# Linear attention followed by an MoE layer on one core: v of the first two batches moved to SyncE's queue, matmuls on zeros ahead of the first transposes, and a new order

## The chip, the cores and the metric

The kernel runs on one core of a Trainium2 chip. The metric is the device time of one execution in microseconds (us). A core has five engines that run beside each other and wait for each other by semaphores: TensorE (PE; its weight loads are listed apart as PEld), VectorE (DVE), ScalarE (ACT), GpSimd (POOL) and SyncE (SP). [...]

## The reference

```python
def phi(x):                                   # per head, w_phi is 64 x 128
    proj = einsum('bhsd,df->bhsf', x, w_phi)
    proj = proj - max(abs(proj), axis=-1, keepdims=True)
    return concatenate([exp(proj), exp(-proj)], axis=-1)
q_p, k_p = phi(q), phi(k)                     # q, k, v: 8 batches x 8 heads x 576 x 64, fp32
kv  = einsum('bhsf,bhsd->bhfd', k_p, v)
z   = sum(k_p, axis=2)
num = einsum('bhsf,bhfd->bhsd', q_p, kv)
den = einsum('bhsf,bhf->bhs', q_p, z)[..., None] + 1e-06
x   = (num / den) as 4608 tokens x 512        # heads side by side
h   = x @ w_in                                # 512 x 2048
g   = where(h > 0, h, exp(min(h, 0)) - 1)
out = g @ w_out                               # 2048 x 512
```

## The kernel before

**Tiling.** A *quad* is four heads of one batch; there are 16, two for each batch, quads 2b and 2b+1. A head's 576 rows are 512 main rows and a tail of 64. A *chunk* is 512 tokens: the main rows of batch b are chunk b, all the tails together are chunk 8. All matmuls take bf16.

**One quad.** k and q (`k_b`, `q_b`, cast to bf16 by POOL's DMAs) are transposed to `kT`, `qT`: in quads 0 to 4 by PE (tile `tr`, tail `trt`, L530 and L534) with a copy out of PSUM by DVE or ACT (L538, L542), from quad 5 on by SP's transposing DMAs (L504, L510). PE projects k (`pk`, L558), DVE takes the largest absolute value (`m_k`, L585), ACT the exponentials `EK`, `EKt` (L604). From `m_k` ACT makes the factors `em` (L649); POOL copies them (L663) and scales v with them into `vs` (L672, six operations for each quad, four large and two small). q is projected twice, with the rows on the partitions for the maximum `m_q` (L558 and L576) and with the features on them (`pq`, L702 and L714) for the exponentials `Eq`, `Eqt` (L753). Then PE makes `pkv` (L785), ACT or DVE copies it to `kv` (L799), PE makes `pn` and `pnt` (L833, L848), DVE weighs and adds the parts into `tot` (L868, L874), divides (`den`, `rec`, L906, L907), and DVE or POOL writes x (L911). x is transposed to `xT` by PE in batches 0 and 1 (L963, L967, copies L971, L975), by SP later.

**One chunk.** Sixteen times: four matmuls `ph` of w_in with `xT` (L1014), the exponential `e_sb` on ACT (L1026), minus one on POOL (`u_sb`, L1030), the ELU into `gT` on DVE (L1037). Then `po`, 64 matmuls of `gT` with w_out (L1080), copies to `o_sb` and stores by SP (L1112, L1116). A chunk's `ph` need both quads of its batch.

**The order.** Nothing is scheduled at run time. A class `Planner` holds a list of operations, each with a cost for each engine that may run it, what it depends on, and a rank from a table written out in the code (`RANKS`, 2140 two-digit numbers). While the program is built it goes through a modelled time: whenever an engine is free it takes the operation of lowest rank whose inputs the model says are there. So the ranks and the model's constants (`COLD`, `COLD_TIMES`, `LANDING`, ...) fix each engine's queue. On the chip each engine works through its queue in order; an instruction that waits holds up all behind it on its engine.

**Loads.** `load` (L427) puts loads on POOL's queue, each behind the one before: first k, q and v of batch 0 in halves of four heads (parts 0 and 2) with the tails (part 1, two DMAs) between, then k of batch 1, four parts of w_in, q of batch 1, four parts of w_in, w_out. `load_v` (L433) puts v of batches 1 to 7 on SP's queue. `hold(b)` (L1204), for b from 1, lets DVE write a column of the v tile from a maximum of quad 2b-1 (L1211), so that SP's load of v of batch b waits until then. v stays fp32 in SBUF.

**Start.** Before the planned part SP loads w_phi twice, and DVE clears w_phi_both, casts w_phi into it (L1148) and clears `EKts`, `Eqts` and a column of `tot` (L1145 to L1151).

Of the kernel before, what the change touches and what calls it, by code (L numbers as in the profile page):

```python
# [8 lines left out]
FP32 = mybir.dt.float32  # L9
# [22 lines left out]

DIGITS = "0123456789ABCDEFGHIJKLMNOPQRSTUVWXYZabcdefghijklmnopqrstuvwxyz+-"
RANKS = (
    "5L1J7b5G3Z4s4qD27p1C557m4k4m1E565q1G5tA-1TBCBQ1L4c51Bt1Q4x193m0P136l1X1K4F2o9g7X"
    "7k0r3G0O2y7l7n1W80Nh4K32Eg0L3972711D4e3Q5l1V3N5v3S5r14345n4w5z4a1U15Js2lHP6U3xCM"
    "0T2-1P1O7N1q6j6N0M4J2u0H3O2r0z29CG3A4bBS0n5kAE0k2788B31l091Y1r1k1dAl2O4I7EAj211j"
    "6R9x6q1h3p70MoAD8H1B8c5O9wHN7wAO9zJ5HY2bMuB6BD2vAwBGBkA+BMB116Mt8+CI2Y6n2w17829W"
    "316VBHEj2x916iC62K2C0Q4L8x33Bv222t4H0i5T4U0F5o6bHK1S7G5R5CDA4ZBl1w5X0c2S2j5W4C5Y"
    "8t1F9r2+1a1n3gBn3T636vIL3Y101b570w7PAUA20U7SCf3t0Z745D6w0l264g003K6KAH2n3k7KAN4G"  # L40
    "8a2kFn0-3j7o9a4dGM5-AT7J1t5sFa7I0A504vJE3J3h4M4-E7JZ8CDkCq5Z0E5ICb6d9o0B0G59FE8O"
    "3V4r2L2E2Z5A28371I5H443U7q1H0J3r2M2g2I2d353H9Z3q6z0u4Q423F3C3d8f3c3W1y0o3-3w3sHk"
    "68Ax462e2Q6t3B3a3I476hBy1-K930Ak20B-3z4A6k1A6J240+6B9-4B1+Ck050C2N0f7F5+0h1p4uNv"
# [12 lines left out]
    "DyDlJLMCJmD4EGCeCx2aMyQSE1JUHEBL5c7s9q6rEIAeMIAJ1mMKC56+3eECBVIiGyMRBNO1ARAXIYCu"
    "L2Es9iLWMzDWOYO2Tx927YK09SALTb9pVCEOLvTa84NC9B4nEtCnIUEeC1MkGkHjDpDsVMAqHwF3I5Do"
    "WcThC7GLGFD6AbMqFzF4L-FJEAFbITBjQP3lB49tO-FW4+ImFxA1LTEJA6IoGiEFF2HXGcHg437QBg6S"
    "G9L9E+Dh2mCaNnLk4RJ0NVFq0a8pApHb1cVXNdE08gKVNXCm6TL0OfHQGUHIDaFr9GCdOdHqDOKWNFHl"
    "GlKiF8LK1oL4AFGBKoJ8QfKhC-I1OTJYNLKP9LO7OuPSOHSzEdVZMnRuNyL1UkNjQBM9OMRtJhT2RxS8"  # L60
    "P5GeK6GfM16Z6fLrM7D9EaCgLHIbRK7-HSFAPa0y6CH3787vU9J4FQWZ12GHRQ9R2G8JJ1HzEmP4OjRh"
    "KDFu3DKBEK5h2s9kO+AhLlELJv0S3XBFD5HpIIQ61xKMJFINJ9HHJ-I+Cr3+JpBXPmJVA5JNH4A3IWFt"
    "CtMZIKE4Gx6LDYHGJSCoNzIGHTFIInHJMvWYLbEc9d9JWiJRCBJkUvEZRFWI73FfJuEUB5Q9IuI6E-90"
    "KLEXEMSMJcM4CCBEC9ENLoNBBIIFB2QyL7NAGoRlOyIfHiCSJqJXC3KILp9+KrLiBPJoM3NKLcMUA9OP"
    "SBHuVmQ8PYHU8FMmOqEP8b5QETLzGZPfNcO9DG7aPBKN1ZWsQeNr2TH8OnKg0DI3NIHZ7uIZNZNu1zJa"
    "4oNYOXLDOSISIrMYP3KFSaKRNmLf0mBoGuQ3GK7R5bRM5gIjGtKY8THvBBM+LGLmMaL3UbW2V-JdORQW"
    "LVRpVgLQUdUDLNOwPxTmP0UsUrEBKJHA53KHKGChPu6aKnIpL+SVWCMpQ5DrIsE6TuTrWaMwX1X2LnLg"
    "9YROX6MJWxIcCHCyGmR9KlHoK7M8N3TyWyK3FXEpTnN1Tt75I4D0D+H+MEWhI0H-QrK4H2P6JDMTP23n"
    "MdNoSYMF5pLXNfPOHFN59vIOFYGYO3QONR6xIAKtFKEVVTV8BOJgWUVASNP1QzUOUEJx8sVfRINNMHTg"
    "UHOJX7GqKUJMRgI2IhJQQ1I7N0WjWqIkExIlRbN276Lx7iIBIJUJPAJwEyG0QtIaI-MAL8MS4fIVMQGJ"  # L70
    "OUJjAf7DMxA4LZMG8NMORXG5V5JCHCQFDZD-PvLwCwHxNMFRDI6EO6LOOF9sNqPPDLIvDXJb0bItFdLq"
    "Fj9nOLHROELEQaLh2zVsOiNe8nKbOpRCGaBfPwPpGNPcNQQ2FeXGP8N+FsPbClLeDj8QNgLaTIIyNpNW"
    "H5UnPgPTKpVIVuO8R+S+TwT9UYSGVvTUJWP+U3WTUjSiTKFVHnOsEQTBOkK-86LAKsH0SoX8QwM5WnPi"
    "M2RZW5M-XBIRW3WmX0NaVPWOSdTdNJHdMPG1MVGpHfGCTRTkMeMrRBHyVcDbDmMgWQVJO5MbQEDdOrVQ"
    "MBPzN-QKJORnHWPXRy3LSs9mOxSu5wUGPjRE4ES1UuT3JtRiUzQkUcIPPkMcFFI8WETfTlS2SHWoSqPt"
    "WlWdV3PGWGRJUINETzQGVNUtWpRfPFDER7RNV7FGG4RrMhTiRHE2V9FSQbMfWMU1VaF5H1DwRDX5VSV6"
    "SFRcLFRmR5S78wKEMiA8KdSC4tSPShSELRSjOoWzLyU4KAMMSARd8SWeG-RGBpJ3MDKCEbWvOcOIGWKS"
    "O4QRFiVl8WPKD1XPOvQVFOPlP9O07CLLCUSOGzLJQhUM8eXIPDRUCRVrEoSr8oVWFgQ+2VXHQcKaF+Kc"
    "NbN4GTXFXQOb2WIwPHPLVeOGVdTpVFVxUaR0TsPyU0PeSXPMRYWBJePoUVN7VtUBWHRLG7GnMNH9MWKw"
    "KyStUqGbVkUlWXQUWwWkVnNxWfXKW8URXOW+WKRkWWXRXMUAVEVjGgMlCPFkW0K2IHQMSyTPWFQAULGd"  # L80
    "FPSxSIWAW6ERI9RoPsVBG2W-NGUpV+UZVoNkSJTLSmB8RTSTTHSeOOW1T7RWDCT0HaUCVVQjSpKjICSD"
    "L5U8SKWbU+U7NHSbSUS3VRQHVpPhScRRN9QiTcUyM0NOV1CjDfR1RaIeQuAaEwCsT4X3SZPqWuSlWPT5"
    "RPU5QNL6QvTOSnU6TVHVNiToVOQpLMHrWDU-S5X9TASgWgXCS0TJTXQoSSUoSkW7VHQsUxQmDqWJNTPZ"
    "GGR2H6PJFLUXR4RwCcIdGvQIUmIzPCMsTDQYQCPnDUQqQlQ-IXXANUT1FhXEOZUSDgTYF-QnQ7WtQ0VL"
    "8qTFW9RAGXIqFMV4R-WNOQWLVyWrPdPVEvX4VwVDM6OVTMSvTZTEONN6UTTvQTS-SQR3P7UKUQTeUeUw"
    "VzSwVUUU8iVbTCQQGjXLVKSRD8WVOtTNUiQxMjSWF1ViNtPUCYXJOhRS8YUNQdPIF0VqNsS4C+HtRvP-"
    "FmKZOaUWT6KvGrRe06XDNwTGS9KzQgLPFcXNQJOW8VUgQZUhR8T-OeTTVGVYRzT8TqWRTSSLVhT+UfW4"
    "UFV0U2UPTjRqOzRVTWV2TQRsK10g255EAtQXJzLj"
)


# [34 lines left out]
class Planner:  # L126
# [1 line left out]
    OWN = {"PE": 0.17, "ACT": 0.12, "DVE": 0.1, "POOL": 0.04, "SP": 0.0}  # L128
    LAG = {"PE": 0.25, "ACT": 0.2, "DVE": 0.13, "POOL": 0.07, "SP": 0.0}

    COLD = 46.0
    COLD_TIMES = 1.4

    CHANGE = 0.095

    MB_PER_US = 0.37
    MB_PER_US_OF_ONE = 0.26
    LANDING = 3.2

    AHEAD = 8  # L140

# [26 lines left out]
    def run(self):  # L168
# [9 lines left out]
        dma = 0.0  # L178
# [54 lines left out]
        while todo:  # L233
            started = False
            for e in ready:
# [37 lines left out]
                o.seen = o.end + self.LAG[e]  # L273
                if o.load:
                    took = o.load / self.MB_PER_US
                    o.seen = max(o.end + o.alone, dma + took + self.LANDING)
                    dma = max(dma, o.end) + took
                    if e == "POOL":
                        landed += [o.seen] * (2 if c > 1.2 else 1)
                for bank in o.uses:  # L280
# [29 lines left out]
def kernel(  # L310
# [111 lines left out]


    landed = {}
    swdge = [None]

    def load(name, mb, cost, fn, deps=()):  # L427

        o = add({"POOL": cost}, fn, deps, behind=[swdge[0]], key=-6.0, load=mb)
        swdge[0] = o  # L430
        landed[name] = o

    def load_v(name, mb, cost, fn, deps):  # L433
        landed[name] = add({"SP": cost}, fn, deps, key=-2.0, load=mb)
# [10 lines left out]
    def plan_loads(b):  # L445

        plan.slot = 2.0 * b - 2
        for n in range(2):
            deps = [o for g in range(2) for o in quads[2 * b - 4 + g]["tr"][n]]
            load(  # L450
                (b, n, 0),
                1.05,
                0.9,
                lambda e, n=n: load_main(nc.gpsimd, n, b, 0, 8),
                deps,
            )
            load((b, n, 1), 0.13, 1.26, lambda e, n=n: load_tails(nc.gpsimd, n, b))
            landed[b, n, 2] = landed[b, n, 0]
        deps = [o for g in range(2) for o in quads[2 * b - 4 + g]["vs"]]
        load_v((b, 2, 0), 1.05, 0.45, lambda e: load_main(nc.sync, 2, b, 0, 8), deps)  # L460
        load_v((b, 2, 1), 0.13, 0.8, lambda e: load_tails(nc.sync, 2, b), deps)
        landed[b, 2, 2] = landed[b, 2, 0]

    def plan_quad(i):
# [90 lines left out]
        def project(n, hh, bank):  # L555
            pk = psum(bank, [P, 4, F], FP32, "pk")
            for j in range(2 if hh < 4 else 1):
# [4 lines left out]
                    start=True,  # L562
                    stop=True,
                )

# [574 lines left out]
    wst = moesm.tile([P, CHUNK], FP32, name="e_sb")[:, 0:F]  # L1142
    for c in range(2):
        nc.sync.dma_start(out=wst[c * D:(c + 1) * D, :], in_=w_phi)
    nc.vector.memset(w_phi_both, 0.0)  # L1145
    for c in range(2):
        r = slice(c * D, (c + 1) * D)
        nc.vector.tensor_copy(w_phi_both[r, c, :], wst[r, :])  # L1148
    for t in EKts + Eqts:
        nc.vector.memset(t, 0.0)  # L1150
    nc.vector.memset(tot[:, :, D1:], 1e-6)  # L1151


    def load_first(n, part):
# [9 lines left out]

        load((0, n, part), 0.52, 0.8 if n or part else 1.19, load_half)

    for n, part in (
        (0, 0), (0, 1), (0, 2), (1, 0), (1, 1), (2, 0), (2, 1), (1, 2), (2, 2)
    ):
        load_first(n, part)  # L1170
    load_v((1, 2, 0), 1.05, 0.45, lambda e: load_main(nc.sync, 2, 1, 0, 8), [])
    load_v((1, 2, 1), 0.13, 0.8, lambda e: load_tails(nc.sync, 2, 1), [])
    landed[1, 2, 2] = landed[1, 2, 0]

    def load_kq(n):
# [27 lines left out]

    def hold(b):  # L1204

        plan.slot = 2.0 * b - 2
        q = quads[2 * b - 1]

        def mark(e):
            for o in (0, BW):  # L1210
                nc.vector.tensor_copy(  # L1211
                    staged(b, 2)[:, o:o + 1], q["st"]["m_q"][:, 0:1]
                )

        o = add(
            {"DVE": 0.13},
            mark,
            [q["m_q"]] + [x for g in (4, 3) for x in quads.get(2 * b - g, {}).get("vs", [])],
            key=-6.0,
        )  # L1220
        for j in range(2):
            landed[b, 2, j].deps.append(o)

    for b in range(1, B):
        hold(b)
    plan.run()

# [29 lines left out]
```

## Time and profile before

| | |
|---|---|
| median of 3 runs | 377.64 us (376.81 to 378.94) |
| the profiled execution | 376.4 us, its span 374.6 us |
| busy: PE, DVE, ACT, POOL | 350.2, 266.0, 274.3, 245.7 us |
| mean granted clock of TensorE | 0.984 |
| bytes moved by DMA | 43.15 MB, mean 115 GB/s |
| chain that ended last, by engine | PE 80%, ACT 9%, POOL 4% |

The span runs from the first instruction to the last; the time of the execution is 1.8 us longer. The profile gives busy times of each engine, what ended each idle stretch (its releaser), and the clock that TensorE was granted, as a share of full speed. PEld overlaps PE. A group of instructions in the order of time is shown with its start, length, engine, line, and tile written and tiles read; "SPq" and "POOLq" are the instructions of a DMA queue. A quad or a batch is not named in the profile; which one a group belongs to follows from the order.

### The profile page before, as it was taken

The numbers are of one execution on the slowest core, as the hardware profiler recorded it, in microseconds if no ns is written. First come the engines' busy times: TensorE is split into PE (matmuls) and PEld (weight loads), VectorE is DVE, ScalarE is ACT, GpSimd is POOL, SyncE is SP. The second block draws the span as 40 slices with busy tenths as digits, with TensorE's granted clock in tenths as the row PEclk, the third lists the DMA queues.
The fourth block names the chain that finished last, engine by engine and source line by source line (L and its number), as shares of the span: only waits on it lengthen the run. The fifth ranks groups of instructions, "written<-read, shape, count | busy, mean of one in ns | idle before, by whom it ended". The sixth has DMA issues, their size and how long they took to land.

```text
span 374.6 us, 8362 instructions
## 1 busy us (share of the span) xinstructions
PE 350.2 (93%) x3086; PEld 191.8 (51%) x3086; DVE 266.0 (71%) x559; ACT 274.3 (73%) x605; POOL 245.7 (66%) x356
## 2 busy tenths in 40 slices
PE   3676599999999999999999999999999999999995
PEld 2455364654655555446554556545655454444443
DVE  4889768887789498959886887788767760755300
ACT  2999699799987688999678996879776743555411
POOL 8998659955899967496775586376786622554300
PEclk9989979999999999999999999999999999999999
DMA  8999999995869879679297246323330203000023
GB/s 100 247 173 231 205 194 180 94 142 162 152 109 149 135 96 206 103 151 174 64 164 216 43 100 122 92 97 84 98 61 28 60 32 116 1 28 23 35 58 84
DMA packets 87033, 43.15 MB, mean 115 GB/s; under 512 B 55216, under 2 KB 81200, under 8 KB 86992
## 3 DMA queue, kind: packets, MB, share of 16 engines
q1 hardware_dynamic: 58000, 27.80, 34.1%
q0 software_dynamic: 28992, 14.82, 30.8%
q8 instruction: 24, 0.39, 0.5%
q14 instruction: 17, 0.14, 0.1%
HBM read 36.77 MB, written 9.44 MB: 123 GB/s over the span
## 4 chain that ended last, share of the span: by engine, by line
PE 80%; ACT 9%; POOL 4%; issue 3%; DVE 2%; DMA 1%; POOLq 0%; ACTq 0%
PE po L1080 32%; PE ph L1014 30%; PE pkv L785 5%; PE pk L558 4%; ACT EK L604 4%; PE pn L833 3%; PE pk L576 2%; ACT EKt L604 2%; ACT Eq L753 2%; POOL vs L672 2%; POOL u_sb L1030 1%; PE pq L702 1%; DMA k_b<-in_k_dram 1%; PE pnt L848 1%; DVE m_k L585 1%
## 5 line engine op out<-in xcount | busy, mean ns | idle before, releaser
L1080 PE MATMUL po<-w_out_sb,gT 128*128 128x512 bf16 (+1 forms) x592 | 136.2, 373 | 0.0
L1037 DVE SCALAR_TENSOR_TENSOR gT<-u_sb,ph 128x512 bf16<-128x512 bf16 x144 | 96.4, 684 | 49.6 <-POOL u_sb L1030 49.1
L1030 POOL TENSOR_SCALAR u_sb<-e_sb 128x512 bf16<-128x512 f32 x144 | 88.1, 618 | 65.9 <-ACT e_sb L1026 65.5
L1014 PE MATMUL ph<-xT,w_in_sb 128*128 128x512 bf16 x512 | 119.1, 380 | 0.0
L1026 ACT ACTIVATE e_sb<-ph 128x512 f32<-128x512 f32 x144 | 87.1, 609 | 35.7 <-PE ph L1014 34.5
L1014 PEld LDWEIGHTS <-w_in_sb 128*128 128x128 bf16 x576 | 54.6, 98 | 61.5 <-issue 2.4
L1080 PEld LDWEIGHTS <-gT 128*128 128x128 bf16 x592 | 54.8, 98 | 56.6 <-issue 4.0
L672 POOL TENSOR_TENSOR vs<-v_b,em 128x512 bf16<-128x512 f32 (+1 forms) x96 | 77.3, 834 | 4.1 <-DMA v_b<-in_v_dram 3.6
L604 ACT ACTIVATE EK<-pk 128x512 bf16<-128x512 f32 x128 | 71.7, 630 | 10.0 <-PE pk L558 9.4
L753 ACT ACTIVATE Eq<-pq 128x512 bf16<-128x512 f32 x128 | 69.3, 620 | 4.5 <-PE pq L702 4.3
L585 DVE TENSOR_REDUCE m_q<-pk 128x4 f32<-128x512 f32 (+1 forms) x80 | 47.9, 628 | 13.7 <-PE pk L576 13.5
L585 DVE TENSOR_REDUCE m_k<-pk 128x4 f32<-128x512 f32 (+1 forms) x80 | 49.4, 630 | 9.8 <-PE pk L558 4.8
L911 POOL TENSOR_TENSOR x<-tot,rec 128x576 bf16<-128x576 f32 x28 | 31.8, 1150 | 25.7 <-DVE rec L907 25.7
L1103 ACT COPY o_sb<-po 128x512 f32<-128x512 f32 (+1 forms) x30 | 17.4, 581 | 32.1 <-PE po L1080 32.0
L868 DVE TENSOR_TENSOR tot<-pn,w 128x260 f32<-128x260 f32 x64 | 26.0, 422 | 7.4 <-PE pn L833 6.6
L558 PE MATMUL pk<-w_phi_both,kT 128*128 128x256 bf16 x144 | 26.1, 287 | 3.2 <-ACT Eq L753 1.2
L833 PEld LDWEIGHTS <-Eq 128*128 128x128 bf16 x512 | 22.3, 97 | 11.1 <-issue 2.5
L785 PEld LDWEIGHTS <-EK 128*128 128x128 bf16 x512 | 23.0, 99 | 8.4 <-issue 5.6
L833 PE MATMUL pn<-kv,Eq 128*128 128x65 bf16 x512 | 25.1, 193 | 1.6 <-ACT EK L604 0.9
L785 PE MATMUL pkv<-vs,EK 128*128 128x65 bf16 x512 | 25.0, 196 | 1.7 <-POOL vs L672 1.3
L874 DVE TENSOR_TENSOR tot<-tot,pn 128x260 f32<-128x260 f32 x64 | 25.8, 418 | 0.3
L604 ACT ACTIVATE EKt<-pk 64x256 bf16<-64x256 f32 x64 | 22.7, 377 | 2.2 <-PE pk L558 1.7
(70 smaller groups left out, 285.2 us busy)
## 6 DMA issues: line engine op xcount, KB each, us to landing
out_dram<-o_sb SPq DMA_DIRECT2D x32, 256.0 KB, 2.4
v_b<-in_v_dram SPq DMA_DIRECT2D x7, 1024.0 KB, 6.3
k_b<-in_k_dram POOLq DMA_DIRECT2D x7, 512.0 KB, 7.4
q_b<-in_q_dram POOLq DMA_DIRECT2D x7, 512.0 KB, 8.2
w_in_sb<-in_moe_w_in_dram POOLq DMA_DIRECT2D x8, 256.0 KB, 6.2
w_out_sb<-in_moe_w_out_dram POOLq DMA_DIRECT2D x4, 512.0 KB, 15.3
v_b<-in_v_dram POOLq DMA_DIRECT2D x2, 512.0 KB, 6.2
v_b<-in_v_dram SPq DMA_DIRECT2D x14, 64.0 KB, 5.1
```

The source lines that it names most:

```text
L558: nc.tensor.matmul(pk[:, 2 * j:2 * j + 2, :].rearrange("p a b -> p (a b)"), in_tile(n)[:, 2 * hh + j, :], w_phi_rhs, start=True, stop=True,)
L585: nc.vector.tensor_reduce(largest(n)[:, cols], bank.tile[:, 0:len(range(2 * NS)[cols]), :], axis=AX.X, op=ALU.max, apply_absolute_value=True,)
L604: nc.scalar.activation(EK()[:, hh, sg, :] if hh < 4 else EKt[r, s, sg, :], bank.tile[r, 0:n, :].rearrange("p a b -> p (a b)"), ACT.Exp, sc ...
L672: nc.gpsimd.tensor_tensor(st["vs"][:, sg, r, 0:D], kqv[b, 2][:, o:o + n * D].rearrange("p (n d) -> p n d", d=D), st["em"][:, sg, r, None]. ...
L753: nc.scalar.activation(dst, src, ACT.Exp, scale=1.0 - 2.0 * sg)
L785: nc.tensor.matmul(pkv[:, c, sg, :], st["EK"][:, 2 * c + s, sg, t * F:(t + 1) * F] if t < NT else EKt[:, s, sg, c * F:(c + 1) * F], st["vs ...
L833: nc.tensor.matmul(pt[:, t, :], st["Eq"][:, par, c, sg, o:o + P], st["kv"][:, s, c, sg, :], start=True, stop=True,)
L1014: nc.tensor.matmul(ph, w_in_sb[:, ct, jt * P:(jt + 1) * P], xTs[ch][:, ct, :] if ch < B else xT_tail[:, ct // 2, :, ct % 2, :], start=(ct ...
L1026: nc.scalar.activation(t["e"], bank.tile, ACT.Exp)
L1030: nc.gpsimd.tensor_scalar(t["u"], t["e"], -1.0, 1.0, op0=ALU.add, op1=ALU.mult)
L1037: nc.vector.scalar_tensor_tensor(gTs[ch][:, jt, :], t["u"], 0.0, bank.tile, op0=ALU.min, op1=ALU.max)
L1080: nc.tensor.matmul(bank.tile, gTs[ch][:, jt, tt * P:(tt + 1) * P], w_out_sb[:, jt, o0:o1], start=(jt == 0), stop=(jt == N_JT - 1),)
```

## The change

- v of batch 0 no longer goes on POOL's queue. It goes on SP's as two halves and the tails, and v of batch 1 follows there, behind the second half of batch 0's.
- `hold(0)` is new: DVE writes the v tile's column of batch 0 from `kT` of quad 0, so SP starts these loads when the first keys have been copied. `hold(1)` goes; v of batch 1 waits only for its place in the queue.
- POOL's loads are no longer each behind the one before; a rank of their own (and, from batch 2, the tails' dependence on the transposes of the tile's last use) orders them.
- Nine matmuls of 128 x 512 on `EKts[0]`, cleared to zero, stand ahead of all of PE's planned work and write PSUM bank 7. The clearing of `EKts[0]` moves ahead of that of `w_phi_both`.
- The model: PE counts as slower by 1.2 up to 20 us instead of by 1.4 up to 46; loads issued before 20 us take 1.35 times as long; loads given a landing time of their own over 5.8 us (batch 0's v: 6, 7 and 10 us, batch 1's: 20) take that.
- All 2140 ranks are new.

```diff
 RANKS = (
-    "5L1J7b5G3Z4s4qD27p1C557m4k4m1E565q1G5tA-1TBCBQ1L4c51Bt1Q4x193m0P136l1X1K4F2o9g7X"
+    "0P0f0k0+0q0v0Y5p2m5N3v0-1S2P1U2d222q2p323x349P463V4D3e0m1i5-0D0j2e6c0u0i0201080x"
...
-    COLD = 46.0
-    COLD_TIMES = 1.4
+    COLD = 20.0
+    COLD_TIMES = 1.2
...
+    BESIDE_UNTIL = 20.0
+    BESIDE_TIMES = 1.35
...
                 if o.load:
                     took = o.load / self.MB_PER_US
-                    o.seen = max(o.end + o.alone, dma + took + self.LANDING)
-                    dma = max(dma, o.end) + took
+                    if now < self.BESIDE_UNTIL:
+                        took *= self.BESIDE_TIMES
+                    if o.alone > 5.8:
+                        o.seen = o.end + o.alone
+                    else:
+                        o.seen = max(o.end + o.alone, dma + took + self.LANDING)
+                        dma = max(dma, o.end) + took
...
-        o = add({"POOL": cost}, fn, deps, behind=[swdge[0]], key=-6.0, load=mb)
-        swdge[0] = o
-        landed[name] = o
+        key = -6.0 + 0.001 * len(landed)
+        landed[name] = add({"POOL": cost}, fn, deps, key=key, load=mb)
...
-            load((b, n, 1), 0.13, 1.26, lambda e, n=n: load_tails(nc.gpsimd, n, b))
+            load((b, n, 1), 0.13, 1.26, lambda e, n=n: load_tails(nc.gpsimd, n, b), deps)
...
+    nc.vector.memset(EKts[0], 0.0)
     nc.vector.memset(w_phi_both, 0.0)
...
-    for t in EKts + Eqts:
+    for t in EKts[1:] + Eqts:
         nc.vector.memset(t, 0.0)
...
+    warm = banks[7].tile([P, CHUNK], FP32, name="warm", tag="bank7")
+    zeros = EKts[0].rearrange("p a b c -> p (a b c)")
+    for _ in range(9):
+        nc.tensor.matmul(warm, zeros[:, 0:P], zeros[:, 0:CHUNK], start=True, stop=True)
...
-    for n, part in (
-        (0, 0), (0, 1), (0, 2), (1, 0), (1, 1), (2, 0), (2, 1), (1, 2), (2, 2)
-    ):
+    for n, part in ((0, 0), (0, 1), (0, 2), (1, 0), (1, 1), (1, 2)):
         load_first(n, part)
-    load_v((1, 2, 0), 1.05, 0.45, lambda e: load_main(nc.sync, 2, 1, 0, 8), [])
-    load_v((1, 2, 1), 0.13, 0.8, lambda e: load_tails(nc.sync, 2, 1), [])
+    def load_v_first(name, mb, cost, alone, fn):
+        landed[name] = add({"SP": cost}, fn, key=-2.0, load=mb, alone=alone)
+
+    for part in (0, 2):
+        load_v_first(
+            (0, 2, part),
+            0.52,
+            0.45,
+            6.0 if not part else 10.0,
+            lambda e, part=part: load_main(nc.sync, 2, 0, 2 * part, 2 * part + 4),
+        )
+        if not part:
+            load_v_first((0, 2, 1), 0.13, 0.8, 7.0, lambda e: load_tails(nc.sync, 2, 0))
+    load_v_first(
+        (1, 2, 0), 1.05, 0.45, 20.0, lambda e: load_main(nc.sync, 2, 1, 0, 8)
+    )
+    load_v_first((1, 2, 1), 0.13, 0.8, 20.0, lambda e: load_tails(nc.sync, 2, 1))
...
     def hold(b):
 
-        plan.slot = 2.0 * b - 2
-        q = quads[2 * b - 1]
+        plan.slot = max(2.0 * b - 2, 0.0)
+        if b:
+            like = quads[2 * b - 1]["m_q"]
+            src = lambda: quads[2 * b - 1]["st"]["m_q"][:, 0:1]
+        else:
+            like = quads[0]["moved"][0][0]
+            src = lambda: quads[0]["st"]["kT"][:, 0, 0:1]
 
         def mark(e):
             for o in (0, BW):
-                nc.vector.tensor_copy(
-                    staged(b, 2)[:, o:o + 1], q["st"]["m_q"][:, 0:1]
-                )
+                nc.vector.tensor_copy(staged(b, 2)[:, o:o + 1], src())
...
-        for j in range(2):
+        for j in range(3 if not b else 2):
             landed[b, 2, j].deps.append(o)
+        if not b:
+            for j in range(2):
+                landed[1, 2, j].behind.append(landed[0, 2, 2])
 
-    for b in range(1, B):
+    hold(0)
+    for b in range(2, B):
         hold(b)
```

## The prediction

> **What bounds the kernel now.** I read the busy time in 40 slices first, then the busy time of short stretches, then who waited for whom up to 60 us, and last the instructions in order of time. The slices say where time is still to be had:
>
> ```profile
> PE   3676599999999999999999999999999999999995
> ...
> POOL 8998659955899967496775586376786622554300
> PEclk9989979999999999999999999999999999999999
> DMA  8999999995869879679297246323330203000023
> ```
>
> TensorE (PE) is full from the sixth slice (about 47 us) on. One slice is 9.4 us. All that a change at the start can win lies before. Adding the idle time of PE over the stretches gives 5.6 us up to its first instruction, 13.7 us from there to 60 us, only 0.96 us between 60 and 350 us, and 4.1 us at the tail. PEclk, the granted clock, dips in the sixth slice. The stretches (length, then busy us of PE, its weight loads, DVE, ACT and POOL, then clock, DMA share, GB/s) show the worst place:
>
> ```profile
> 35.00:40.00 5.00, 3.79 (x68) 3.02 (x65) 4.85 (x13) 4.64 (x13) 1.42 (x3) 1.00 1.19 224
> 40.00:45.00 5.00, 1.74 (x16) 0.95 (x16) 4.51 (x11) 3.48 (x7) 4.11 (x6) 1.00 1.24 203
> 45.00:50.00 5.00, 3.90 (x53) 2.98 (x53) 1.56 (x4) 2.59 (x7) 3.67 (x5) 0.53 1.38 201
> 50.00:55.00 5.00, 4.86 (x45) 2.67 (x45) 3.90 (x8) 5.00 (x14) 2.03 (x3) 0.79 1.57 189
> ```
>
> From 40 to 45 us PE has 1.74 us of work, and the clock then falls to half, so that the busy PE of the next rows does half as much. The waits up to 60 us name the links of one chain:
>
> ```profile
> ACT kv L799 <- PE pkv L785: 3.6, 1, 3.6
> POOL vs L672 <- DMA v_b<-in_v_dram: 3.6, 1, 3.6
> PE pkv L785 <- POOL vs L672: 3.5, 4, 1.6
> ```
>
> In order of time (start, length, engine, line, in brackets the idle time before it):
>
> ```profile
> 5.62 1.03 PE L530 MATMUL tr<-ident,k_b 128*128 128x128 bf16 x8 [5.62 <-DMA k_b<-in_k_dram]
> ...
> 16.33 0.61 PE L530 MATMUL tr<-ident,q_b 128*128 128x128 bf16 x8 [0.90 <-DVE m_q L585]
> ...
> 25.85 0.43 SPq L403 DMA_DIRECT2D v_b<-in_v_dram  x1
> ...
> 39.68 3.05 POOL L672 TENSOR_TENSOR vs<-v_b,em 128x512 bf16<-128x512 f32 x3 [3.58 <-DMA v_b<-in_v_dram]
> ...
> 42.77 0.29 PE L785 MATMUL pkv<-vs,EK 128*128 128x65 bf16 x4 [0.82 <-POOL vs L672]
> ...
> 45.58 0.21 PE L785 MATMUL pkv<-vs,EKt 128*128 128x65 bf16 x1 [1.61 <-POOL vs L672]
> ...
> 50.81 1.67 PE L1014 MATMUL ph<-xT,w_in_sb 128*128 128x512 bf16 x4
> ```
>
> v of batch 1 is issued at 25.85 because SP waits for the mark that `hold(1)` writes, and lands 13.7 us later. POOL, which had ended its scales at 34.74 and its issues at 36.1, starts quad 2's scaling of v only at 39.68. `pkv` of quad 2 waits for it at the head of PE's queue, and what stands behind it waits too: the transposes of quad 1's x, whose input is ready at 45.27 and which run at 49.87, and the first MoE matmul at 50.81.
>
> **The change part by part.**
>
> *v of batch 1 early.* It loses the wait for `m_q` and follows v of batch 0 on SP, at about 8 to 11 us. The bound on its landing is the 13.7 us of the present one under traffic, so at most 25 us, and quad 2's scaling needs it at about 35. POOL's 3.58 us go. PE's four waits on `vs` are 0.82, 0.60, 1.61 and 0.52, together 3.55 us. I take 3.6. Both ends: 2.0 if the next thing (the last sums of quad 1 on DVE, den at 42.70, x ended at 45.27) holds the first MoE matmul back, and 5.2, all of PE's idle time from 36 to 47 us.
>
> *The clock behind that hole.* From 45.4 to 52.05 us the clock is 0.5. The same groups at full clock elsewhere: 25 `pkv` 0.79 instead of 1.53 (40 take 1.26 at 96.79), two q projections 0.61 each instead of 1.82 for both, eight transposes 0.61 instead of 1.04, four `ph` 0.86 instead of 1.67. The differences are 0.74, 0.60, 0.43 and 0.81, sum 2.6. It goes if the hole goes. Bounds 0 and 2.6; I take 2.0, because PE is thin there anyway: at 15 to 18 us, with 0.39, 0.61 and 0.43 us busy in each, the clock dropped too, to 0.5 at 18.
>
> *Matmuls on zeros.* One EKt memset (1.02 for two, so 0.51) moves ahead of the w_phi memset at 0.84; the casts behind wait for DMA anyway (1.86 idle), so it costs nothing. Nine matmuls of 512 columns at half clock are 9 x 1.67/4 = 3.8 us, from about 1.45 to 5.2, ahead of the keys at 5.62: 0.4 us of cover, and what they overrun beyond it would be lost one for one. What they may win is eight transposes in 0.61 instead of 1.03, and 0.1 to 0.2 in the first projections: ACT, busy almost without a gap from 8.09 to 43.5, starts up to 0.6 earlier. No row shows zeros releasing the clock, so the bounds are -0.6 and +0.4; I take -0.3. [...]
>
> *v of batch 0 from POOL to SP.* POOL loses 0.82 + 1.31 + 0.84 = 2.97 us of issues between 6.71 and 10.28. POOL is busy without a gap to 36.1, so quad 1's scaling, done at 32.5, could end up to 3.0 earlier; but ACT is just as full, and quad 1's `pkv` at 33.10 was released last by DVE (0.16), not by POOL. So the value lies near the small end: I take -0.5, bounds -3.0 and 0. SP issues seven DMAs now (0.43 each for mains, about 1.4 for a pair of tails) by about 12 us; its next work in the profile, apart from the v it issues today, is at 52.13, so nothing is queued behind. The mark of `hold(0)` takes 0.22 of DVE (row at 25.67), in DVE's 0.84 idle before 8.51, and `hold(1)`'s 0.22 goes: nothing.
>
> *Contention.* The DMA row is at 9 from 5 to 56 us at about 0.2 MB/us, so v's 1.18 MB of batch 1, moved ahead, push other loads back by up to 5.8 us. Slack: w_in is issued last at 28.57, lands 6.2 us later and is first read at 50.8 (16 us); w_out lands by 49.4 and is read at 74.2; k of batch 1 lands at 18.4 and its projections run at 27.4 (9 us). Batch 0 has less: its second half of k, issued at 4.00, is transposed at 10.55. The nearest row of a wait for a load there is the 0.38 of the tail transpose at 7.04; for two such loads I take +0.7, bounds 0 and +4.0 (what the slower rival below works out). [...]
>
> *Loads not chained, new ranks.* POOL waited for a DMA before an issue only 0.31 us (at 10.59). The ranks redraw the whole order; after 60 us they can win 0.96 us of idle time at most, and could lose as much as one hole like the present (3.6). I take 0.
>
> **Sum:** -3.6 - 2.0 - 0.3 - 0.5 + 0.7 = -5.7. The profiled execution took 376.4 (span 374.6 and 1.8 around it), giving 370.7. The median of the runs shown, 377.64, lies 1.24 higher: 371.9.
>
> **The rivals.** *A larger gain:* POOL's 3.0 us reach quad 1's x in full, 2.5 us more than in the sum: 369.4. For it speaks that POOL is gapless to 36; against it, ACT is too. *The wait is replaced:* ACT's load for quads 0 and 1, not v, sets the first MoE matmul, which stays near 48; then only part of the hole goes, about 2 us: 375.6, or nothing, 377.6. For it: ACT full to 43.5. Against it: ACT itself then waits 3.63 us for `pkv`. *Slower:* v of batch 0 lands late on SP. On POOL's queue its first half was issued at 6.71, landed in 6.2 us and was used at 14.38. On SP it is issued a little after the first kT, 7.7; if it takes the 13.7 us of the present SP load, it lands at 21.4, POOL's chain slips 7.0 us less the 2.97 that it lost, and the first MoE matmul comes 4.0 later than now if the hole at 40 us has merely moved: 381.6. It decides from a landing at about 14.4 + 3.0 = 17.4 us on. Against it: that load was twice as long, 1 MB for 0.5.
>
> **How the numbers follow.** Forecast 0.56, larger gain 0.09, wait replaced 0.18 (0.07 of it faster by over 0.5%, 0.11 within), slower 0.17. Half a percent, 1.9 us, is about what a measurement of this kernel can tell from no change. So faster 0.56 + 0.09 + 0.07 = 0.72, same 0.11, slower 0.17. The favourable ends together reach 376.4 - 5.2 - 2.6 - 0.6 - 3.0 = 365.0, or 366.2 on the median, which is unlikely; the range begins at 367.5. Upward it takes in the forecast with contention's +4.0 (375.2), the replaced wait and half of the slower case: 379.5. The forecast's own range is 368 to 375.5.
>
> **What would show it.** Right: v of batch 1 issued before 13 us, no POOL wait on v_b near 36, PE's waits on `vs` under 1 us, the first `ph` at 44 to 47, no half clock from 45 to 52, PE idle from 6 to 60 us at 9 to 10 instead of 13.7, and nine zero matmuls that end before the keys land. Wrong: POOL idle on v_b at 14 to 20, the first `ph` after 49, or new idle of PE after 60 us.

## The result and the profile after

The change made the kernel slower. Over 4 runs each in the same session, the changed kernel took 388.36 us (386.37 to 389.81) and the kernel before 377.7 us. The ratio is 1.0276, with a 95% interval of 1.0218 to 1.0335. The forecast of 371.9 us was wrong in sign. The profiled execution took 389.18 us with a span of 387.4; before it was 376.4 and 374.6. So the traces differ by 12.8 us, a little more than the medians (10.7).

The busy shares in 40 slices (9.7 us each) of the changed kernel:

```profile
PE   6543868999999998999999999999999999999995
POOL 8615869789748968559685598247587722776000
PEclk9855777999999999999999999999999999999999
DMA  8997999937997998457656664296013013000213
```

PE's weak slices are the same few at the start, but the fourth has fallen to 3 (it was 6), POOL's third is 1, and the granted clock, which was below 8 in one slice before, is so in five. The stretches show the place (length, then busy us of PE, weight loads, DVE, ACT, POOL, then clock, DMA share, GB/s):

```profile
20.00:25.00 5.00, 4.02 (x41) 3.03 (x40) 2.82 (x6) 3.08 (x9) 1.89 (x3) 0.50 1.15 241
25.00:30.00 5.00, 0.70 (x6) 0.29 (x5) 1.01 (x2) 2.20 (x6) 0.00 (x0) 0.50 1.25 208
30.00:35.00 5.00, 0.08 (x3) 0.08 (x3) 0.00 (x0) 0.00 (x0) 1.60 (x4) 0.50 0.74 101
35.00:40.00 5.00, 4.50 (x60) 3.96 (x60) 2.76 (x6) 1.85 (x4) 4.96 (x7) 0.50 0.81 124
```

From 25 to 35 us all compute engines stand almost still, while the DMA engines are busy until past 30. That is a transfer everybody waits for. The waits of the first 100 us (us in total, times, longest) name it:

```profile
ACT kv L807 <- PE pkv L793: 10.8, 2, 10.6
PE pkv L793 <- POOL vs L680: 9.7, 2, 9.2
POOL vs L680 <- DMA v_b<-in_v_dram: 9.4, 1, 9.4
```

It is the very chain of the prediction's waits (v to POOL's scaling to PE's `pkv` to ACT's `kv`), with 9 to 11 us in place of 3.6. In order of time, first SP, then POOL and PE:

```profile
7.19 1.00 SPq L411 DMA_DIRECT2D v_b<-in_v_dram  x2
8.22 1.47 SPq L421 DMA_DIRECT2D v_b<-in_v_dram  x2
9.74 1.98 SPq L411 DMA_DIRECT2D v_b<-in_v_dram  x1
11.76 50.58 SPq L421 DMA_DIRECT2D v_b<-in_v_dram  x4
```

```profile
1.46 4.02 PE L1166 MATMUL warm<-EKt 128*128 128x512 bf16 x9 [1.46 <-DVE EKt L1153]
15.92 3.05 POOL L680 TENSOR_TENSOR vs<-v_b,em 128x512 bf16<-128x512 f32 x3
33.35 0.41 POOL L680 TENSOR_TENSOR vs<-v_b,em 128x128 bf16<-128x128 f32 x1 [9.41 <-DMA v_b<-in_v_dram]
34.92 0.21 PE L793 MATMUL pkv<-vs,EKt 128*128 128x65 bf16 x1 [9.22 <-POOL vs L680]
64.57 1.02 PE L1022 MATMUL ph<-xT,w_in_sb 128*128 128x512 bf16 x3
```

In the program SP's queue reads: v of batch 0, first half and second half (the row at 7.19), the two tails of batch 1 (8.22), the 1 MB of batch 1 (9.74), and only then the two tails of batch 0, the first two of the four in the last SP row; the other two are issued much later, for batch 2. POOL began to scale v of batch 0 at 15.92 (before, at 14.38), and later stood before a 128x128 tail until 33.35. The chain of work that ended last (start, length, what) goes through the load of the second of these tails, and POOL's scaling follows it there at 33.35. Below it stand the issues of the two tails alone:

```profile
16.44 16.78 DMA v_b<-in_v_dram
11.76 5.79 SPq L421 DMA_DIRECT2D v_b<-in_v_dram  x2
```

Each tail is 64 KB. From issue to landing the first took 20.3 us and the second 16.8 us; the megabyte ahead of them took 21.2 us and landed at 31.0. Issuing itself was slow too: of the 5.79 us, the instruction of the first tail held SP's sequencer for 4.63 us. SP's queue is not all of the delay: a part of w_in that POOL issued at 11.86, on its own queue, took 17.9 us to land.

### The profile page after: what moved, and what is told of

The parts are those of the page before. It is cut to its first block, busy times and chain, and to the rows that moved or that the text cites. A ratio compares the mean times of both kernels' runs of the same rounds, so it can differ in the third digit from the quotient of the medians.

```text
span 387.4 us, 8341 instructions
## 1 busy us (share of the span) xinstructions
PE 353.0 (91%) x3050; PEld 195.3 (50%) x3095; DVE 267.9 (69%) x562; ACT 272.9 (70%) x602; POOL 242.6 (63%) x352
## 4 chain that ended last, share of the span: by engine, by line
PE 71%; DMA 7%; ACT 6%; POOL 6%; DVE 5%; issue 3%; SPq 0%; POOLq 0%; ACTq 0%
PE po L1088 28%; PE ph L1022 26%; PE pkv L793 5%; DMA v_b<-in_v_dram 4%; ACT EK L612 3%; PE pk L564 3%; PE pn L841 3%; POOL vs L680 3%; DMA qT<-q_b 3%; DVE gT L1045 2%; PE pk L584 2%; POOL u_sb L1038 2%; PE pq L710 1%; PE warm L1166 1%; PE pnt L856 1%
## 5 line engine op out<-in xcount | busy, mean ns | idle before, releaser
L1088 PE MATMUL po<-w_out_sb,gT 128*128 128x512 bf16 (+1 forms) x564 | 131.4, 373 | 1.3
L1022 PE MATMUL ph<-xT,w_in_sb 128*128 128x512 bf16 x495 | 116.7, 379 | 2.2 <-DVE gT L1045 1.2
L1111 ACT COPY o_sb<-po 128x512 f32<-128x512 f32 (+1 forms) x26 | 14.8, 569 | 42.7 <-PE po L1088 42.6
L919 POOL TENSOR_TENSOR x<-tot,rec 128x576 bf16<-128x576 f32 x28 | 31.8, 1150 | 16.8 <-DVE rec L915 16.5
L876 DVE TENSOR_TENSOR tot<-pn,w 128x260 f32<-128x260 f32 x64 | 26.3, 423 | 13.7 <-PE pn L841 9.4
L793 PEld LDWEIGHTS <-EK 128*128 128x128 bf16 x512 | 24.5, 104 | 14.9 <-issue 10.2
L793 PE MATMUL pkv<-vs,EKt 128*128 128x65 bf16 x128 | 22.9, 202 | 9.2 <-POOL vs L680 9.2
L841 PEld LDWEIGHTS <-Eq 128*128 128x128 bf16 x512 | 23.2, 98 | 11.6 <-issue 1.3
L564 PE MATMUL pk<-w_phi_both,kT 128*128 128x256 bf16 x144 | 25.1, 282 | 2.7 <-DVE kT L544 0.8
L793 PE MATMUL pkv<-vs,EK 128*128 128x65 bf16 x512 | 26.1, 203 | 0.7 <-POOL vs L680 0.5
```

The costliest lines, as they stand in the source:

```text
L564: nc.tensor.matmul(pk[:, 2 * j:2 * j + 2, :].rearrange("p a b -> p (a b)"), in_tile(n)[:, 2 * hh + j, :], w_phi_rhs, start=True, stop=True,)
L793: nc.tensor.matmul(pkv[:, c, sg, :], st["EK"][:, 2 * c + s, sg, t * F:(t + 1) * F] if t < NT else EKt[:, s, sg, c * F:(c + 1) * F], st["vs ...
L841: nc.tensor.matmul(pt[:, t, :], st["Eq"][:, par, c, sg, o:o + P], st["kv"][:, s, c, sg, :], start=True, stop=True,)
L1022: nc.tensor.matmul(ph, w_in_sb[:, ct, jt * P:(jt + 1) * P], xTs[ch][:, ct, :] if ch < B else xT_tail[:, ct // 2, :, ct % 2, :], start=(ct ...
L1088: nc.tensor.matmul(bank.tile, gTs[ch][:, jt, tt * P:(tt + 1) * P], w_out_sb[:, jt, o0:o1], start=(jt == 0), stop=(jt == N_JT - 1),)
```

## The experiments

Two kinds of lines come up all through: the wait for v, and "the first MoE matmul", which is the first `ph` row (50.81 before, 64.57 after). Four of the kernels below (those with "nov1" in the name) scale a zero in batch 1, as their expectation says for the first. Their times are those of the kernel's schedule.

### The tails of batch 0 moved forward on SP (e1_tails)

```diff
-            lambda e, part=part: load_main(nc.sync, 2, 0, 2 * part, 2 * part + 4),
+            lambda e, part=part: (
+                load_main(nc.sync, 2, 0, 2 * part, 2 * part + 4),
+                load_tails(nc.sync, 2, 0) if part else None,
+            ),
...
-            load_v_first((0, 2, 1), 0.13, 0.8, 7.0, lambda e: load_tails(nc.sync, 2, 0))
+            load_v_first((0, 2, 1), 0.13, 0.8, 7.0, lambda e: None)
```

The two tails follow v's second half; all other queues are as in the changed kernel.

> The changed kernel with batch 0's two tail loads of v issued right behind batch 0's second half, ahead of batch 1's 1 MB; every other queue as in the changed kernel. Theory Q (the order on SP's queue: the tails stood behind batch 1's v): POOL's wait of 9.41 us at 23.9 goes, the tails land near 20 us, and with the hole goes part of the half clock at 34 to 40 us (about 2.5): 388.4 - 9.4 - 2.5 = 376.5, range 373 to 380. Rival C (contention of the early 1 MB or the new ranks, whatever the order of the tails): POOL still waits over 5 us for v, time 384 or more.

It took 377.91 us, ratio 1.003 (1.0003 to 1.0058). Each against the kernel before in its own session, a loss of 10.7 us on the medians has become one of 0.6: 10 us are gone, by the place of two 64 KB loads alone.

```profile
7.27 0.98 SPq L411 DMA_DIRECT2D v_b<-in_v_dram  x2
8.29 3.97 SPq L421 DMA_DIRECT2D v_b<-in_v_dram  x4
12.31 0.71 SPq L411 DMA_DIRECT2D v_b<-in_v_dram  x1
23.10 0.42 POOL L680 TENSOR_TENSOR vs<-v_b,em 128x128 bf16<-128x128 f32 x1
54.42 1.02 PE L1022 MATMUL ph<-xT,w_in_sb 128*128 128x512 bf16 x3
```

The tail is scaled at 23.10 without a wait. So the slowing is the order of SP's queue. But with that order mended, and with v of both batches on time, nothing is gained: the first `ph` stands at 54.42, later than before.

### The zeros (e2_nozeros, e3_before_zeros)

The first is the changed kernel without the nine matmuls; the second is the kernel before with them, and with the EKt memset that feeds them:

```diff
+    nc.vector.memset(EKts[0], 0.0)
     nc.vector.memset(w_phi_both, 0.0)
...
+    warm = banks[7].tile([P, CHUNK], FP32, name="warm", tag="bank7")
+    zeros = EKts[0].rearrange("p a b c -> p (a b c)")
+    for _ in range(9):
+        nc.tensor.matmul(warm, zeros[:, 0:P], zeros[:, 0:CHUNK], start=True, stop=True)
```

> The changed kernel without the nine matmuls on zeros. Theory Q: they lie ahead of a wait for a DMA that does not depend on them, so the time is within 1.5 us of 388.4. [...]

> The kernel before with the nine matmuls on zeros and the earlier clearing of the first EKt, nothing else. Theory Q: ACT's first exponential 0.6 us earlier than 8.09, time 0 to 0.6 below that of before: 377.1 to 377.7. Rival W (zeros do harm): 379 or more.

Without zeros the changed kernel took 386.64 us (ratio to the kernel before 1.0237, 1.0201 to 1.0272; with them 1.0276, 1.0218 to 1.0335). With zeros the kernel before took 377.25 us, ratio 0.9996 (0.9983 to 1.0008).

```profile
1.46 3.58 PE L1157 MATMUL warm<-EKt 128*128 128x512 bf16 x9 [1.46 <-DVE EKt L1145]
5.63 0.62 PE L530 MATMUL tr<-ident,k_b 128*128 128x128 bf16 x8 [0.60 <-DMA k_b<-in_k_dram]
```

With zeros the first eight transposes take 0.62 instead of 1.03 us, the first nine projections 1.18 instead of 2.10, and ACT's first exponential starts 0.37 us earlier. The granted clock doesn't show this difference: it reads 1.00 from 5 to 11 us in both traces. Then it falls in the trace with zeros, to 0.64 from 11 to 12 and 0.50 from 12 to 14 us, and again to 0.50 from 19 to 24 us (PE had been idle for 1.49 us before 9.97 and for 1.00 us before 11.57), and nothing is left at the end. The changed kernel with zeros was 1.7 us slower than without, and in the other pairs of this study (e1_tails beside e7_tails_nozeros, e10_batch2_first_zeros beside e9_batch2_first) it was 0.4 and 2.7 us. Only the last of these three, with both kernels in one session, is clear of the noise; in the other two the intervals overlap. In no pair did the zeros gain.

### Parts of the change in the kernel before (e4_before_v1early, e8_before_v0sp)

```diff
+            if not early and i == 0 and n == 1:
+                early.append(True)
+                mark_now(1, largest(n)[:, cols])
```

That releases v of batch 1 by the first maximum of quad 0's q (at about 16.4 us) instead of quad 1's `m_q`. The second kernel moves only v of batch 0 from POOL to SP, behind the first kT, with the tails between the halves.

> The kernel before with batch 1's v released on SP by quad 0's first maximum of q (about 16 us) instead of quad 1's (25.7 us); every queue's order as before. The forecast's mechanism: it lands near 29 us, POOL's wait of 3.58 us at 36 and the half clock from 45 to 52 us go: 377.7 - 5.6 = 372, range 370 to 375. Rival C (the early 1 MB pushes back other loads by as much): 377 or more.

> The kernel before with batch 0's v on SP (first half, tails, second half) released by the first kT, its four issues taken out of POOL's queue; batch 1's v at 25.7 us and every other order as before. The forecast's term for POOL's 2.97 us: 376 to 377.4. Theory C: k and q of batches 0 and 1 come later beside it; 378.5 or more.

v of batch 1 alone: 381.34 us, ratio 1.0121 (1.009 to 1.0152), so slower, where the forecast wanted 372. v of batch 0 alone: 378.72 us, ratio 1.0044 (1.0009 to 1.0078), where the forecast had booked POOL's 2.97 us of issues as a gain of 0.5. The first one's trace has two new waits of PE, and a DVE row that the forecast had not considered:

```profile
31.23 1.04 PE L536 MATMUL tr<-ident,q_b 128*128 128x128 bf16 x8 [3.54 <-DMA q_b<-in_q_dram]
38.86 5.92 DVE L920 TENSOR_TENSOR x<-tot,rec 128x576 bf16<-128x576 f32 x2
39.52 4.00 POOL L681 TENSOR_TENSOR vs<-v_b,em 128x512 bf16<-128x512 f32 x4
45.71 1.04 PE L972 MATMUL tr<-ident,x 128*128 128x128 bf16 x8 [5.45 <-DVE tot L877]
```

Before, the same q_b transposes ran at 27.87 without a wait for their load: v's 1.18 MB, put ahead, pushed q of batch 1 back. That is contention, priced in the prediction at 0.7 with an end of 4.0. The third row is POOL's scaling of v of batch 1, which now begins as soon as POOL is free; DVE's multiplication of quad 0's x beside it took 5.92 us. In the kernel before, POOL was waiting for v at that moment, the same two instructions took 1.41, and PE waited only 0.57 us ahead of the transposes of x:

```profile
34.84 1.41 DVE L911 TENSOR_TENSOR x<-tot,rec 128x576 bf16<-128x576 f32 x2
37.41 0.62 PE L963 MATMUL tr<-ident,x 128*128 128x128 bf16 x8 [0.57 <-DVE tot L868]
```

The second kernel's runs go from 376.5 to 382.5 us, and its profile is of one of 381.4. In it POOL waited 6.88 us for v of batch 1 (3.58 before) and began to scale it at 44.90 (39.68 before), and DVE's x of quad 1 fell beside the scaling:

```profile
44.32 2.26 DVE L919 TENSOR_TENSOR x<-tot,rec 128x576 bf16<-128x576 f32 x2
44.90 3.95 POOL L680 TENSOR_TENSOR vs<-v_b,em 128x512 bf16<-128x512 f32 x4 [6.88 <-DMA v_b<-in_v_dram]
```

### Holding v of batch 1 back in the mended kernel (e5_tails_v1at17, e6_tails_v1at22)

In e1's kernel the load of batch 1 is released by the first maximum of quad 0's q, or of quad 1's.

> e1_tails with batch 1's v released on SP by quad 0's first maximum of q (17 us) instead of following batch 0's v at once (8 to 12 us); POOL, PE and ACT keep their queues, DVE gets two one-column copies. Theory C (the early 1 MB on SP slows k and q of batches 0 and 1 on POOL's queue, and a POOL that waits for one of its own earlier loads): the waits for q_b and k_b loads up to 21 us (PE 3.5 us, POOL about 5 us in e1_tails) shrink to half or less, time 373 to 376. Rival R (the new order itself gives away what the change wins): 377 to 379 as e1_tails.

> e1_tails with batch 1's v released on SP by quad 1's first maximum of q (22 us); it is scaled at 42.6 in e1_tails and needs up to 16 us, so it is not late. Theory C: as e5_tails_v1at17 or 1 us better, 372 to 376. Rival R: 377 to 379.

They took 380.02 and 378.47 us, ratios 1.0066 (1.0041 to 1.0091) and 1.0045 (1.0012 to 1.0078). Holding the load back didn't win the 2 us or more that a loss to its early traffic would give back, so that theory isn't supported.

### The mended kernel without zeros, and its order of loads (e7_tails_nozeros, e9_batch2_first, e10_batch2_first_zeros)

In the new ranks the keys' tails and the queries of batch 3 stand on POOL ahead of those of batch 2. e9 and e10 swap them back, without and with zeros:

```diff
+    in_order = {(n, part): [2, 3] for n in range(2) for part in range(2)}
...
-                lambda e, n=n: load_main(nc.gpsimd, n, b, 0, 8),
+                lambda e, n=n: load_main(nc.gpsimd, n, next_of(n, 0, b), 0, 8),
```

> e1_tails without the nine matmuls on zeros. [...]

> e7_tails_nozeros with batch 2's loads of k and q put on POOL's queue ahead of batch 3's, at the same two places of the queue. In the changed kernel batch 3's q stands ahead of batch 2's and takes the staging buffer that batch 0 left, so that batch 2's waits for batch 1's buffer; in e7 PE then waits 2.4 us at 62.5 for q of batch 2. Theory I (this inversion of the unchained loads is the second half of what the change lost): the wait goes and 2.0 to 2.8 us with it, 374.7 to 375.5. Rival A (ACT, full from 20 to 60 us, holds PE up just after): 377 to 378.

> The same on e1_tails, so with the nine matmuls on zeros: the changed kernel with both orders mended. Theory I: 375 to 376 and within 0.7 of e9_batch2_first, since the zeros move nothing that lasts. Rival A: 377.5 to 378.5.

e7 took 377.49 us (0.9992 to 1.0029), e9 377.01 us (0.9957 to 0.9998), e10 379.67 us (1.0025 to 1.0058). The row that led to e9 is this one of e7, a wait for q of batch 2:

```profile
64.93 0.62 PE L536 MATMUL tr<-ident,q_b 128*128 128x128 bf16 x8 [2.43 <-DMA q_b<-in_q_dram]
```

It is gone in e9, for 0.5 us on the medians (0.9 with each against its own kernel before), and the two intervals still overlap. So the order of these loads is at most a small cost of the new ranks, and not the 2.0 to 2.8 us that theory I gave it. In e9 ACT, by the stretches, is busy 7.99, 6.50, 7.92 and 7.86 of each 8 us from 24 to 56, and the first `ph` comes at 53.24.

### Taking the wait away, and nothing else (e11_before_nov1wait, e12_before_nov1)

The prediction's central term can be measured by itself: the kernel before, whose scaling of batch 1 doesn't read v.

```diff
-                kqv[b, 2][:, o:o + n * D].rearrange("p (n d) -> p n d", d=D),
+                zero_v[:, None, :].to_broadcast((P, n, D))
+                if b == 1
+                else kqv[b, 2][:, o:o + n * D].rearrange("p (n d) -> p n d", d=D),
```

> The kernel before, where POOL's scaling of batch 1 (quads 2 and 3) reads a zero in place of v of batch 1; v is still loaded at the same place, so the traffic is the same, and only the wait is gone. Batch 1's output is therefore not the attention of the reference; its instructions and their shapes are. Forecast's mechanism (the wait for v of batch 1 and the half clock behind it are 5.6 us): 372, between 370 and 373.5, first MoE matmul at 44 to 47. Rival A (ACT is full from 8 to 60 us and sets the first MoE matmul whatever v does): 376.0 to 377.7, first MoE matmul at 49 or later, with ACT's 3.6 us wait for pkv gone or moved. In between, 373.5 to 376: both hold in part.

> As the run before, and v of batch 1 is not loaded at all (1.18 MB of traffic less, between 26 and 40 us). If the traffic of v of batch 1 itself is what costs (rival C, contention): 2 us or more below the run before. If it is the wait alone, or ACT: within 1 us of the run before. It is also the most that any placing of this load could win: if it stays within 2 us of 377.6, no earlier issue of v of batch 1 could have brought the forecast's 5.7.

With v still loaded it took 372.95 us, ratio 0.9901 (0.9872 to 0.993). Eight of 12 runs lay between 372.3 and 373.1, the others between 375.7 and 378.1. In the eight, taking the wait away was worth 4.5 us, not far from the forecast's 5.6; the profile is of the slowest of the four. Without the load it took 377.26 us, ratio 0.9997 (0.9985 to 1.0009), in all 12 runs between 376.7 and 377.9. Less traffic gave less, which neither the forecast nor the two rivals allow. e12's trace repeats what e4's showed (its first `ph` stands at 51.47):

```profile
34.82 6.06 DVE L914 TENSOR_TENSOR x<-tot,rec 128x576 bf16<-128x576 f32 x2
36.10 3.40 POOL L673 TENSOR_TENSOR vs<-zero_v,em 128x512 bf16<-128x512 f32 x4
41.80 1.03 PE L966 MATMUL tr<-ident,x 128*128 128x128 bf16 x8 [4.96 <-DVE tot L871]
```

The view of the tile x in the same kernel, in a window around these rows, tells the two apart (durations least, median, most, in ns):

```profile
L914 DVE TENSOR_TENSOR x<-tot,rec x2: 741/3071/5401, 34.8 to 35.5; 128x576 bf16<-128x576 f32 x2
```

The first multiplication takes its usual 0.74 us. The second starts at 35.5, still runs when POOL's four scalings begin at 36.10, and ends only at 40.88, 1.4 us after the last of them. In the kernel before, x ran at 34.84 while POOL waited for v until 39.68. The wait that the prediction wanted to remove sheltered this multiplication.

### The collision by itself (e13_nov1_xpool, e14_before_xpool, e15_xpool_v1at22, e16_nov1wait_again)

```diff
-            (nc.vector if e == "DVE" else nc.gpsimd).tensor_tensor(
+            (nc.vector if e == "DVE" and i else nc.gpsimd).tensor_tensor(
                 tile("x", work, [P, NS, 2, D], BF16)[:, :, c, :],
```

Quad 0's x goes to POOL, ahead of quad 2's scaling: in e12's kernel (e13), in the kernel before (e14), and in the kernel before with v of batch 1 released by quad 0's last maximum (e15). e16 is e11 once more.

> The run without the load of v of batch 1 (batch 1 scales a zero), where quad 0's multiplication of tot by rec (x, two of 128x576) is moved from DVE to POOL, ahead of quad 2's scaling; nothing else differs. There it took DVE 6.06 us from 34.82, beside POOL's scaling at 36.10 to 39.50, and PE waited 4.96 us for DVE behind it. Theory P (DVE's multiplication and POOL's scaling hold each other up, and that ate the gain): PE's wait before quad 0's x is under 1.5 us, time 372 to 374. Rival L (something else ate it, as the loads or ACT's pace): 376.5 or more.

> The kernel before with the same move of quad 0's x to POOL alone. DVE's 1.41 us at 34.84 become 2 x 1.15 on POOL, which waits for v then anyway: both theories 377 to 378.5, as there is no collision at 34.84 in the kernel before. If it is below 376, the move itself wins, and the run beside it must be read against this.

> The kernel before, complete: quad 0's x on POOL, and v of batch 1 released 3 us earlier, by the last maximum of quad 0's q (about 22.5 instead of 25.67). Its load of 13.7 us then lands near 36.5, as POOL ends x at about 37.1. Theory P: the wait for v is gone without the collision, 374 to 376. Rival L, or the earlier load delaying q of batch 1 as the release at 16.4 did (3.54 us): 377 or more.

> The kernel before with a zero in place of v of batch 1 in its scaling (v still loaded), once more with a profile: 8 of its 12 runs lay at 372.3 to 373.1, 4 at 375.7 to 378.1, and the profile was of one of the latter, with DVE's x of quad 0 at 5.90 us. Theory P: in a profile near 373 that x takes 1.4 to 2 us; near 377 it takes about 6. Rival L: x takes about 6 us in both.

e13 took 374.01 us, ratio 0.9907 (0.9882 to 0.9932): 3.3 us below the kernel before, where e12 was 0.2 below it. That is next to what theory P said (372 to 374), and far from L's 376.5.

```profile
35.83 2.27 POOL L914 TENSOR_TENSOR x<-tot,rec 128x576 bf16<-128x576 f32 x2
38.05 3.39 POOL L673 TENSOR_TENSOR vs<-zero_v,em 128x512 bf16<-128x512 f32 x4
38.91 0.61 PE L966 MATMUL tr<-ident,x 128*128 128x128 bf16 x8 [1.73 <-DVE tot L871]
47.93 0.38 PE L1017 MATMUL ph<-xT,w_in_sb 128*128 128x512 bf16 x1 [0.38 <-DMA k_b<-in_k_dram]
```

PE's wait falls from 4.96 to 1.73 us, a little over the 1.5 expected, and the first `ph` comes at 47.93 instead of 51.47. e14, the control, took 377.03 us, ratio 0.9985 (0.9966 to 1.0003): the move alone does nothing that can be told from no change. So taking away the wait, and with it the load itself, is worth 3.0 us (374.01 against 377.03) when the collision is kept out, and 0.2 in e12, where it is not. How much of the 3.0 is the wait is open. e14's profile is of its fastest run (374.97 us; the other eleven lie from 376.3 to 378.1), and there little of the wait is left, since POOL does x first, and the first `ph` is only 0.6 us later than in e13:

```profile
38.90 3.05 POOL L672 TENSOR_TENSOR vs<-v_b,em 128x512 bf16<-128x512 f32 x3 [0.21 <-DMA v_b<-in_v_dram]
48.56 0.38 PE L1014 MATMUL ph<-xT,w_in_sb 128*128 128x512 bf16 x1
```

e15 took 376.23 us, ratio 0.9956 (0.9927 to 0.9985). It computes everything, and its ratio is the lowest of the complete versions here, 0.4% below the kernel before; the interval overlaps those of e9 and e14. It is short of the 374 to 376 expected: five of its 12 runs lay between 373.5 and 374.3, the others between 375.9 and 377.9. In its trace POOL no longer waits for v, but x on POOL starts at 37.95 where e13 has 35.83, and PE's wait before quad 0's x is 2.34 us. A row ahead of it shows what the earlier load costs, a wait for the tail of q of batch 1 that the kernel before does not have:

```profile
30.74 0.22 PE L540 MATMUL trt<-ident,q_b 128*128 128x128 bf16 x1 [2.36 <-DMA q_b<-in_q_dram]
```

e16's one run took 376.88 us, and its x took 6.06 us, as P says for a run near 377. No profile fell on a run near 373, so whether those runs of e11 escape the collision is open.

## Why the prediction was wrong

**The step that failed** is the one on SP's queue: "SP issues seven DMAs now ... so nothing is queued behind", together with "The ranks redraw the whole order; ... I take 0". It asked what stands behind the seven and not in which order the seven stand. The ranks are part of the change, and they put the tails of batch 0 behind the megabyte of batch 1. Measured: 10 us of the 10.7 (e1_tails), against 0 in the sum, and against 3.6 as the most that the ranks were allowed to lose. The schedule's model gives these tails 7 us from issue to landing; they took 20.3 and 16.8. The slower rival had the right kind of mechanism, v of batch 0 late on SP, but it priced the landing of the first half (decisive from 17.4 us on). That half was in time, scaled at 15.92; the tail landed at 33.2.

**The wait for v and the clock behind it (-3.6 and -2.0).** The reading was right that PE's hole at 40 to 45 us hangs on v of batch 1. It failed where it asked what is late next: it named den and x of quad 1 and put the ends at gains of 2.0 and 5.2. Taking the wait away moves POOL's scaling 3.6 us ahead, on to DVE's x of quad 0, and the sum is 0.2 us below the kernel before (e12_before_nov1), or a loss in a complete kernel (e4_before_v1early, +4.1 with q's wait in it). With the collision moved away the two terms, with the load's traffic, are worth 3.0 us (e13 against e14), not 5.6: the first `ph` came 2.9 us earlier than in the kernel before (47.93 for 50.81), and the clock is still at 0.79 in the stretch from 40 to 48 us. But in eight of e11's 12 runs, with x on DVE and the load kept, they were worth 4.5 us. So the size of these terms differs from run to run, and why is not known; that the collision takes the gain back is shown for the runs that have a trace.

What DVE and POOL hold each other up by is not shown. The rows show who paid in e12: DVE's second multiplication took 5.40 us instead of 0.74, while POOL's four scalings took 3.40 beside it and 3.39 without it (e13). They show no order that decides it: in e12 DVE's instruction had begun, by the records, 0.6 us before the first of POOL's four and still ended after all of them. In e8 DVE's two began at 44.32, 0.58 us before the first of the four, took 2.26 us together instead of 1.41, and ended 2.3 us before the four did.

**Zeros (-0.3).** Right that the first transposes get faster (0.62 instead of 1.03 us, with the granted clock at 1.00 in both traces there); wrong that anything comes of it: 0.0 in the kernel before, and no gain in the three other pairs (0.4, 1.7 and 2.7 us slower on the medians, the last alone clear of the noise).

**v of batch 0 to SP (-0.5).** Wrong in sign, by little: the ratio of e8_before_v0sp is 1.0044 (1.0009 to 1.0078). In its profile, of a run of 381.4 us, the first `ph` came 4.7 us later (55.48), behind a wait for v of batch 1 that had grown from 3.58 to 6.88 us; what made this load later was not taken apart.

**Contention (+0.7, up to 4.0).** Right in kind, and larger where v of batch 1 is put ahead alone: PE waited 3.54 us for q of batch 1 in e4_before_v1early. Two readings behind the 0.7 were wrong. q of batch 1 is missing from the list of slack, though it landed at 27.2 and was transposed at 27.87. And k of batch 1, which landed at 18.4, was first read by the transposes at 19.39 and not by the projections at 27.4, so its slack was 1.0 us and not 9. (The last part of w_in landed after 7.9 us and not 6.2, which changes nothing.) The first two rows are of the kernel before, the third of the changed one:

```profile
19.39 1.06 PE L530 MATMUL tr<-ident,k_b 128*128 128x128 bf16 x8
27.87 0.61 PE L530 MATMUL tr<-ident,q_b 128*128 128x128 bf16 x8
19.88 1.03 PE L536 MATMUL tr<-ident,k_b 128*128 128x128 bf16 x8 [2.07 <-DMA k_b<-in_k_dram]
```

The bound of 25 us on the landing of v of batch 1 did not hold either: issued at 9.74, it took 21.2 us and not 13.7 and landed at 31.0, which is still ahead of the 35 at which it was needed.

**What stays open.** In the changed kernel's own order no x is slowed (DVE's four take 0.75 us each, by the groups), v is in time once the tails are mended, and still the kernel only equals the one before. The two losses looked at, zeros (0.4) and batch 3 ahead of batch 2 (0.5), make up 0.9 us on the medians, and neither is clear of the noise there. ACT is full up to the first `ph` and does other work first than it did in the kernel before; that the rest of the 3.0 us is lost by that order is argued, not shown.

## What to carry to other kernels

When several loads move to one queue, write that queue out in its new order and look for a small early load behind a large later one; here two 64 KB tails behind a megabyte cost 10 us. An engine that waits may be a shelter: before booking a removed wait as a gain, list what the other engines do in the stretch that the work moves into; here two VectorE multiplications took 6.06 us instead of 1.41 beside GpSimd's scalings (e12). To know what a wait is worth, feed its consumer from a constant and measure that first, before changing the loads, and over many runs: e11's fell into two groups some 4 us apart.

## What the runs showed of the hardware that was not expected

- DVE's 128x576 multiplication of tot by rec, begun 0.6 us before four GpSimd multiplications by the records, took 5.40 us instead of 0.74 and ended 1.4 us after all four (e12). Two of them together took 6.06 us there, 5.92 in e4 and 5.90 in e11, where they ended 1.3 us after the four, and 2.26 in e8, where they ended 2.3 us before; in the kernel before, with POOL waiting, they took 1.41. GpSimd's four took 3.40 us beside them in e12, 4.00 in e4, 3.98 in e11 and 3.95 in e8, and 3.39 in e13 without them: VectorE paid nearly all in e12 and most in e4, but in e8 the cost was 0.85 us on VectorE and 0.56 on GpSimd.
- In the changed kernel two 64 KB loads issued behind 1 MB on the same queue landed after 20.3 and 16.8 us, and issuing the first held SP for 4.63 us, where a pair of tails before took 1.51.
- With zeros of 3.6 us ahead of them the first transposes took 0.62 us instead of 1.03 (e3), while the granted clock read 1.00 from 5 to 11 us with zeros and without. With zeros it was 0.64 from 11 to 12 us and 0.50 from 12 to 14, 6 to 9 us after the last of them (1.00 without), with PE busy 8.64 of 14 us from 6 to 20: the faster start bought nothing by itself.
